# Top-32 attention and an ELU feed-forward block: the distance from threshold to largest score is formed on GpSimd in steps 0 to 7 as well

## The chip, the cores and the metric

The kernel runs on one core of a Trainium2 chip. The core's engines run beside each other and wait for one another by semaphores: PE (TensorE, matrix products and transposes; PEld is its weight load), DVE (VectorE), ACT (ScalarE), POOL (GpSimd) and SP (SyncE, which here only starts DMA transfers). Each engine works off its own instructions strictly in the order in which they stand in its queue. The metric is the device time of one execution in microseconds.

## The reference

Eight batches of eight heads, 576 positions, head dimension 64, float32. In every row of scores only the 32 largest take part in the softmax. The heads are then laid side by side as a (4608, 512) matrix, which goes through a feed-forward block of width 2048 with an ELU between its two products.

```python
scores = scale * np.matmul(q, k.transpose(0, 1, 3, 2))
kth = np.partition(scores, -top_k, axis=-1)[..., -top_k:-top_k + 1]
scores = np.where(scores >= kth, scores, -1000000000.0)
scores = scores - np.max(scores, axis=-1, keepdims=True)
attn = np.exp(scores)
attn = attn / (np.sum(attn, axis=-1, keepdims=True) + 1e-09)
attn_out = np.matmul(attn, v)
x = attn_out.transpose(0, 2, 1, 3).reshape(B * S, H * D)
h = x @ w_in
g = np.where(h > 0.0, h, np.exp(np.minimum(h, 0.0)) - 1.0)
out = g @ w_out
```

The weights arrive as float64 and are turned into float32 on the chip.

## The kernel before

**Steps.** The attention is cut into 144 steps. A step takes up to 128 query rows of two heads (the last 64 rows of a batch are paired over four heads), so that it has two rows of work, i = 0 and 1, each a tile of 128 x 576 scores. A step goes through these stations:

- `scores` (L302, L310): PE forms the scores in PSUM, ACT copies them scaled to `sc`. This runs two steps ahead.
- `select_row` (steps 0 to 7: L321, L325, L331) or `select` (later: L344, L349, L356): DVE finds the 32 largest of each row with four `max` instructions of eight values each, and three `match_replace` between them that blot out what was found. The first `max` leaves the largest score in `u.first`, the last one the threshold, the 32nd largest, in `u.last`.
- `mask` (L374 to L376): the gap, threshold minus largest score, one number per partition, is formed in a 128x1 tile. Then ACT applies a Prelu with the threshold as bias (L375) and an exponential with the gap as bias (L376). The two together give exp(score - largest) above the threshold and 0 below it; the exponential also sums the row into `den`.
- `normalise` (L386 to L393): POOL forms the reciprocal of the sum with five small instructions and scales both rows.
- `turn` (L412, L413): PE transposes the weights, ACT copies them to `et`. `attend` and `finish` (L438, L465): PE multiplies with v, and ACT copies the result to `xT`.

When all heads of a block of tokens are there, its feed-forward work is cut into pieces: `hidden` (L510 on PE, L520, L523 and L525 on ACT, the -1 of the ELU in L482 on DVE) and `project` (L535 on PE). `feed` hands them out four times a step by a running account of cost and due time.

**Weights.** `decode_piece` turns the 32 pieces of the weights into float32. A piece passes four stages in successive calls: ACT (L173, L174), then a clamp on POOL (L179) and the sign on ACT (L182), then a shift on DVE (L188), then an add on POOL (L192). SP loads the raw piece three calls ahead (L153) into one of seven buffers, so that each load waits for an add that frees its buffer. `hook` runs one call; `select_row` calls it twice per row, that is four times a step, so that decoding lies almost wholly in steps 0 to 7, with the rest in step 8.

**Order.** In steps 0 to 7 (`n < tight`, with tight = 8) a step's two rows come one after the other. For each the program issues: the first two `max`, for row 1 the normalisation and the transposes of the step before, a share of feed-forward pieces, the rest of the selection with its two decode calls, and then `mask` for that same row. These instructions are not bound to that order: the Tile framework's planner arranges the instructions of each engine by program order and by when their inputs are ready. From step 8 on (`manual_schedule` at L688) the order written in the program is kept on PE, ACT, DVE and POOL; there `mask` belongs to the step before, and its two rows are called at L697 and L705.

`mask` takes the engine that forms the gap as an argument, with GpSimd as default. The call in steps 0 to 7 (L684) passes VectorE; the two later calls pass nothing. Gap tiles have four buffers, so a gap can be written once the exponential four gaps before has read its own.

Of the kernel before, what the change touches and what calls it, by code (L numbers as in the profile page):

```python
# [9 lines left out]
ALU = mybir.AluOpType  # L10
# [71 lines left out]
def kernel(  # L82
# [9 lines left out]
    nc = tc.nc  # L92
# [191 lines left out]
    def turn_qk(whole=False):  # L284
        while turning:
            if next(turning[0], turning) is turning:
                turning.pop(0)
            elif not whole:
                return
# [3 lines left out]
    def scores(u):  # L293

        u.sc = scpool.tile([P, 2, S], FP32, tag="sc", name="sc")
        q0 = QUERIES + u.t.qt * P
        for half in range(2):
            for h, i, rows in u.heads:
                kq = kqT[u.t.b, h // 2]
                part = slice(i * D, (i + 1) * D)  # L300
                k0 = (KEYS if i == 0 else 0) + half * HS
                nc.tensor.matmul(  # L302
                    wide[i][rows, half, 0:HS],
                    kq[part, q0 : q0 + u.t.ql],
                    kq[part, k0 : k0 + HS],
                    start=True,
                    stop=True,
                )
        for i in range(2):
            nc.scalar.activation(  # L310
                u.sc[:, i, :].rearrange("p (a s) -> p a s", a=2),
                wide[i][:, :, 0:HS], AF.Copy, scale=scale,
            )

    def select_row(u, i):
        if i == 0:
            u.first = small.tile([P, 2, 8], FP32, tag="m1", name="m1")
            u.last = small.tile([P, 2, 8], FP32, tag="m4", name="m4")
        sc = u.sc[:, i, :]
        m = u.first[:, i, :]  # L320
        nc.vector.max(m, sc)  # L321
        wk = wkpool.tile([P, S], FP32, tag=f"wk{i}", name="wk")
        cur = sc
        for r in range(TOP_K // 8 - 1):
            nc.vector.match_replace(wk[:], m, cur, TAKEN)  # L325
            cur = wk[:]
            if r < TOP_K // 8 - 2:
                m = small.tile([P, 8], FP32, tag=f"m{i}", name="m")[:]
            else:
                m = u.last[:, i, :]  # L330
            nc.vector.max(m, cur)  # L331
            if r > 0:
                hook()
            if r != 1:
                yield
# [21 lines left out]
            hook()  # L357
            yield

    def mask(u, i, engine=nc.gpsimd):  # L360

        if u.masked:
            return
        if i == 0:
            u.den = small.tile([P, 2], FP32, tag="den", name="den")  # L370
        u.masked = i == 1
        sc, low, top = u.sc[:, i, :], u.last[:, i, 7:8], u.first[:, i, 0:1]
        gap = small.tile([P, 1], FP32, tag="gap", name="gap")
        engine.tensor_tensor(gap[:], low, top, ALU.subtract)  # L374
        nc.scalar.activation(sc, sc, AF.Prelu, scale=-1.0, bias=low, alpha=1.0 / STEEP)  # L375
        nc.scalar.activation(  # L376
            sc, sc, AF.Exp, scale=-STEEP, bias=gap[:], accum_out=u.den[:, i : i + 1]
        )

    def normalise(u):  # L380

        if u.normal:
            return
        u.normal = True
        den = small.tile([P, 2], FP32, tag="dene", name="dene")
        nc.gpsimd.tensor_scalar_add(den[:], u.den[:], EPS)  # L386
        rec = small.tile([P, 2], FP32, tag="rec", name="rec")
        nc.gpsimd.tensor_tensor(rec[:], den[:], power[:], ALU.pow)
        nc.gpsimd.tensor_tensor(den[:], den[:], rec[:], ALU.mult)
        nc.gpsimd.tensor_scalar(den[:], den[:], -1.0, 2.0, ALU.mult, ALU.add)  # L390
        nc.gpsimd.tensor_tensor(rec[:], rec[:], den[:], ALU.mult)
        for i in range(2):
            nc.gpsimd.tensor_scalar(  # L393
                u.sc[:, i, :], u.sc[:, i, :], rec[:, i : i + 1], 1.0, ALU.mult, ALU.mult
            )
# [26 lines left out]
    def attend(g):  # L422
        t = g.tiles[0]
        ps = ps_t.tile([P, JP], FP32, tag="t", name="avps")
        n = P if t.rem else sum(x.ql for x in g.tiles)
        for k in range(2 if t.rem else 1):
            hp = 2 * g.hp + k if t.rem else g.hp
            vt = vT[t.b, hp]
            for c in range(J + 1):
                for i in range(2):  # L430
                    chunk = J if c == J else i * (J + 1) + c
                    w = g.et[:, chunk, :, :].rearrange("p a q -> p (a q)")
                    cols = slice(0, n)
                    if t.rem:
                        c0 = R * (k if i == 0 else 1 - k)
                        w = w[:, c0 : c0 + R]
                        cols = slice(k * R, (k + 1) * R)
                    nc.tensor.matmul(  # L438
                        ps[i * D : (i + 1) * D, cols],
                        vt[:, 2 * J + i if c == J else i * J + c, :],  # L440
                        w,
                        start=(c == 0),
                        stop=(c == J),
                    )
        if t.rem:
            finish(t.block, 2, slice(2 * g.hp, 2 * g.hp + 2), t.cols,
                   ps[:, 0:n].rearrange("p (a q) -> p a q", a=2))
            return
        c0 = 0
        tiles = list(g.tiles)  # L450
        while tiles:
            blk, lo, parts = tiles[0].block, tiles[0].cols.start, 0
            while tiles and tiles[0].block is blk:
                parts += 1
                hi = tiles.pop(0).cols.stop
            finish(blk, parts, g.hp, slice(lo, hi), ps[:, c0 : c0 + hi - lo])
            c0 += hi - lo
# [165 lines left out]
    def feed(n, share):  # L623

        place[0] += 1
        close_gates(2)
        fed["at"] = max(fed["at"], n)
        ahead = [(w - fed["sum"]) / (x - fed["at"]) for x, w in due if x > fed["at"]]
        if ahead:
            fed["over"] += max(0.0, share * min(ahead))  # L630
        fed["at"] += share
        while ffn and decoded[0] >= ffn[0][1] and 0.5 * ffn[0][0] <= fed["over"]:
            cost, _, piece = ffn.pop(0)
            fed["over"] -= cost
            fed["sum"] += cost
            piece()
# [22 lines left out]
    def step(n):  # L659
        return steps[n] if 0 <= n < NS else None  # L660
# [3 lines left out]
    for n in range(NS + 3):  # L664
        for fn, args in todo.pop(n, []):
            fn(*args)
        ahead, cur, prev, done = step(n + 2), step(n), step(n - 1), step(n - 2)
        if n < tight:
            turn_qk(True)
            scores(ahead)  # L670
            for i in range(2):
                passes = select_row(cur, i)
                next(passes)
                if i == 0:
                    while closing:
                        attend(closing.pop(0))
                elif prev:
                    normalise(prev)
                    turn(prev, main)
                    turn(prev, rest)  # L680
                    turn(prev, other)
                feed(n, 0.25)
                next(passes)
                mask(cur, i, nc.vector)  # L684
                feed(n, 0.25)
            continue
        if n == tight:
            ctx.enter_context(tc.manual_schedule(engines=engines))  # L688
        passes = select(cur) if cur else iter(range(4))
        if ahead:  # L690
            scores(ahead)
        while closing:
            attend(closing.pop(0))
        next(passes)
        feed(n, 0.25)
        if prev:
            mask(prev, 0)  # L697
        turn_qk()
        next(passes)
        feed(n, 0.25)  # L700
        if done:
            turn(done, main)
            turn(done, rest)
        if prev:
            mask(prev, 1)  # L705
        next(passes)
        feed(n, 0.25)
        if done:
            turn(done, other)
        next(passes)  # L710
        if prev:
            normalise(prev)
        feed(n, 0.25)
        turn_qk(True)
# [36 lines left out]
```

## Time and profile before

| | us |
|---|---|
| median of four runs | 1664.47 (1663.52 to 1665.56) |
| the profiled execution | 1665.56 |
| its span, first to last instruction | 1663.8 |
| busy: PE, DVE, ACT, POOL | 1594.7, 1504.3, 1163.5, 579.2 |
| gaps (L374) on DVE: 16, from 25.9 to 127.4 | 8.33 busy |
| gaps (L374) on POOL: 272, from 149.9 to 1570.9 | median 0.191 each |

In the lines that follow, times are microseconds from the start of the span unless marked ns. A line of the stage table gives the stretch, its length, the busy time and the number of instructions of PE, PEld, DVE, ACT and POOL, then the granted TensorE clock as a share of full speed, the mean busy share of the DMA engines, and GB/s. A line of waits reads: engine and line that waited, whom for, total us, times, longest. A line of the chain has start, length and what ran; a line of the timeline has start, length, engine, line, operation, output and input, and in brackets the idle time before it with what ended it. A group of instructions of a line gives the durations in ns as min/median/max.

### The profile page before, as it was taken

How to read it: one execution, taken by the hardware profiler on the slowest of the kernel's cores; microseconds unless marked ns; L12 is line 12 of the kernel's file. 1: busy time of each engine (PE TensorE's matmuls, PEld its weight loads, DVE VectorE, ACT ScalarE, POOL GpSimd, SP SyncE). 2: the span in 40 equal slices, each digit the busy share in tenths (PEclk: the TensorE clock that was granted, in tenths of full speed). 3: DMA queues.
4: the chain of work that ended last, by engine and by line, in shares of the span. 5: the costliest groups of instructions: out<-in, count | busy, mean ns of one | idle time of the engine just before them, and what ended most of it. 6: DMA issues, size and time to landing. Idle time of an engine off the chain costs nothing.

```text
span 1663.8 us, 25650 instructions
## 1 busy us (share of the span) xinstructions
PE 1594.7 (96%) x8528; PEld 1031.1 (62%) x8528; DVE 1504.3 (90%) x3060; ACT 1163.5 (70%) x2377; POOL 579.2 (35%) x1415
## 2 busy tenths in 40 slices
PE   5579999999999999999999999999999999999999
PEld 3366777667574767656566676755557575755564
DVE  5898999999999999999999999999999999998500
ACT  5998777668685867678667676768758585857521
POOL 2775333333333333333333233333333333332200
PEclk9678999999999999999999999999999999999999
DMA  7540110001100210011100111001200101000000
GB/s 212 177 138 7 29 48 25 7 15 44 48 1 7 50 37 22 1 28 37 42 14 1 50 32 32 1 15 42 50 13 1 29 14 29 7 7 7 7 13 13
DMA packets 101124, 56.19 MB, mean 34 GB/s; under 512 B 84096, under 2 KB 92288, under 8 KB 100992
## 3 DMA queue, kind: packets, MB, share of 16 engines
q1 hardware_dynamic: 99792, 54.26, 11.7%
q8 instruction: 68, 1.11, 0.3%
q14 instruction: 64, 0.52, 0.1%
q10 hardware_dynamic: 1200, 0.30, 0.1%
HBM read 45.09 MB, written 9.44 MB: 33 GB/s over the span
## 4 chain that ended last, share of the span: by engine, by line
PE 62%; DVE 27%; ACT 5%; issue 1%; POOL 0%; DVEq 0%; ACTq 0%
PE ops L535 22%; PE hps L510 21%; DVE wk L349 12%; DVE m L356 10%; PE avps L438 7%; PE scps L302 6%; PE eps L412 5%; DVE m L344 3%; DVE gT L482 1%; PE qkps L272 1%; ACT sc L376 1%; PE scps L412 1%; ACT sc L375 1%; ACT et L413 1%; ACT raw L182 0%
## 5 line engine op out<-in xcount | busy, mean ns | idle before, releaser
L356 DVE MAX8 m<-wk 128x8 f32<-128x576 f32 x816 | 575.0, 746 | 0.0
L510 PE MATMUL hps<-xT,w_in 128*128 128x256 f32 (+2 forms) x2432 | 547.6, 374 | 12.8 <-ACT xT L465 10.7
L535 PE MATMUL ops<-w_out,gT 128*128 128x512 f32 x1152 | 523.0, 598 | 0.0
L510 PEld LDWEIGHTS hps<-xT,w_in 128*128 128x128 f32 x2432 | 405.9, 193 | 109.5 <-issue 24.2
L349 DVE MATCH_REPLACE8 wk<-m,wk 128x576 f32<-128x576 f32 x544 | 399.5, 741 | 0.0
L535 PEld LDWEIGHTS ops<-w_out,gT 128*128 128x128 f32 x1152 | 208.6, 190 | 233.1 <-issue 220.9
L386 POOL TENSOR_SCALAR dene<-den 128x2 f32<-128x2 f32 x144 | 35.4, 246 | 807.8 <-ACT sc L376 807.5
L375 ACT ACTIVATE sc<-sc,m 128x576 f32<-128x576 f32 x288 | 226.8, 788 | 39.6 <-DVE m L356 39.4
L376 ACT ACTIVATE sc<-sc,gap 128x576 f32<-128x576 f32 x288 | 224.0, 778 | 37.0 <-POOL gap L374 13.6
L310 ACT ACTIVATE sc<-scps 128x576 f32<-128x576 f32 x288 | 174.0, 659 | 77.2 <-PE scps L302 77.1
L393 POOL TENSOR_SCALAR sc<-sc,rec 128x576 f32<-128x576 f32 x288 | 220.7, 777 | 14.9
L302 PE MATMUL scps<-kqT 64*128 64x288 f32 (+1 forms) x1280 | 203.1, 441 | 19.3 <-ACT et L413 9.0
L413 ACT COPY et<-eps 128x512 f32<-128x512 f32 x288 | 166.8, 580 | 70.5 <-PE eps L412 70.2
L438 PE MATMUL avps<-et,vT 128*64 128x256 f32 (+2 forms) x2080 | 195.8, 330 | 4.7 <-ACT et L413 4.4
L349 DVE MATCH_REPLACE8 wk<-m,sc 128x576 f32<-128x576 f32 x272 | 199.8, 742 | 0.0
L412 PEld LDWEIGHTS eps<-ident,sc 128*128 128x128 f32 x1152 | 143.2, 143 | 81.6 <-issue 49.3
L344 DVE MAX8 m<-sc 128x8 f32<-128x576 f32 x272 | 191.1, 743 | 0.0
L482 DVE SCALAR_TENSOR_TENSOR gT<-n,gT 128x512 f32<-128x512 f32 (+1 forms) x132 | 99.8, 756 | 100.6 <-ACT n L525 100.6
L412 PE MATMUL eps<-ident,sc 128*128 128x128 f32 x1152 | 175.2, 277 | 13.6 <-POOL sc L393 11.8
L438 PEld LDWEIGHTS avps<-et,vT 128*64 128x64 f32 x2080 | 123.6, 142 | 80.7 <-issue 27.0
L302 PEld LDWEIGHTS scps<-kqT 64*128 64x128 f32 (+1 forms) x1280 | 108.2, 182 | 90.8 <-issue 44.7
L520 ACT ACTIVATE n<-hps 128x512 f32<-128x512 f32 (+1 forms) x156 | 88.1, 565 | 80.1 <-PE hps L510 76.6
(50 smaller groups left out, 1117.9 us busy)
## 6 DMA issues: line engine op xcount, KB each, us to landing
kin<-in_k_dram SPq DMA_DIRECT2D x64, 128.0 KB, 2.9
raw<-in_moe_w_in_dram SPq DMA_DIRECT2D x16, 512.0 KB, 5.1
vT<-in_v_dram SPq DMA_DIRECT2D x64, 128.0 KB, 2.3
raw<-in_moe_w_out_dram SPq DMA_DIRECT2D x16, 512.0 KB, 3.5
out_dram<-osb SPq DMA_DIRECT2D x32, 256.0 KB, 2.3
qin<-in_q_dram SPq DMA_DIRECT2D x62, 128.0 KB, 2.9
kin<-in_k_dram SPq DMA_DIRECT2D x32, 32.0 KB, 2.6
vT<-in_v_dram SPq DMA_DIRECT2D x64, 16.0 KB, 2.2
```

The source lines that it names most:

```text
L302: nc.tensor.matmul(wide[i][rows, half, 0:HS], kq[part, q0 : q0 + u.t.ql], kq[part, k0 : k0 + HS], start=True, stop=True,)
L344: nc.vector.max(found[i], cur[i])
L349: nc.vector.match_replace(wk[i], found[i], cur[i], TAKEN)
L356: nc.vector.max(found[i], cur[i])
L375: nc.scalar.activation(sc, sc, AF.Prelu, scale=-1.0, bias=low, alpha=1.0 / STEEP)
L376: nc.scalar.activation(sc, sc, AF.Exp, scale=-STEEP, bias=gap[:], accum_out=u.den[:, i : i + 1])
L393: nc.gpsimd.tensor_scalar(u.sc[:, i, :], u.sc[:, i, :], rec[:, i : i + 1], 1.0, ALU.mult, ALU.mult)
L412: nc.tensor.transpose(ps[:, c * P : (c + 1) * P], sc[:, c0 : c0 + P], ident[:])
L413: nc.scalar.copy(g.et[:, chunks, u.at, :], ps[:, 0 : n * P].rearrange("p (c q) -> p c q", c=n),)
L438: nc.tensor.matmul(ps[i * D : (i + 1) * D, cols], vt[:, 2 * J + i if c == J else i * J + c, :], w, start=(c == 0), stop=(c == J),)
L510: nc.tensor.matmul(blk.h[:, f % bank, :], w_in[:, i, f * P : (f + 1) * P], blk.xT[:, i, 0:n_tok], start=(i == 0), stop=(i == NC - 1),)
L535: nc.tensor.matmul(blk.o[:], blk.gT[f // NG][:, f % NG, s * P : (s + 1) * P], w_out[:, f, :], start=(f == 0), stop=(f == NF - 1),)
```

## The change

The call in steps 0 to 7 no longer names an engine, and the argument is gone: all 288 gaps are formed on GpSimd. Sixteen 128x1 subtractions (two rows in each of eight steps) go from DVE's queue to POOL's. Nothing is computed differently.

```diff
-    def mask(u, i, engine=nc.gpsimd):
+    def mask(u, i):
...
         gap = small.tile([P, 1], FP32, tag="gap", name="gap")
-        engine.tensor_tensor(gap[:], low, top, ALU.subtract)
+        nc.gpsimd.tensor_tensor(gap[:], low, top, ALU.subtract)
         nc.scalar.activation(sc, sc, AF.Prelu, scale=-1.0, bias=low, alpha=1.0 / STEEP)
         nc.scalar.activation(
             sc, sc, AF.Exp, scale=-STEEP, bias=gap[:], accum_out=u.den[:, i : i + 1]
         )
...
                 feed(n, 0.25)
                 next(passes)
-                mask(cur, i, nc.vector)
+                mask(cur, i)
                 feed(n, 0.25)
```

## The prediction

> **What bounds the kernel now.** I read the page's busy times first, then busy time by stage, then the waits of the stage in which the edited instructions run, then the chain of work that ended last.
>
> ```profile
> PE 1594.7 (96%) x8528; PEld 1031.1 (62%) x8528; DVE 1504.3 (90%) x3060; ACT 1163.5 (70%) x2377; POOL 579.2 (35%) x1415
> ```
>
> Averages put PE first, but the edit touches only steps 0 to 7, and the instructions of its line tell where these lie:
>
> ```profile
> L374 POOL TENSOR_TENSOR gap<-m,m x272: 182/191/887, 149.9 to 1570.9; 128x1 f32<-128x1 f32 x136
> L374 DVE TENSOR_TENSOR gap<-m,m x16: 143/152/1266, 25.9 to 127.4; 128x1 f32<-128x1 f32 x16
> ```
>
> 272 of the 288 gaps are on POOL already; the 16 that move run from 25.9 to 127.4 us. The table of stages (busy us of PE, PEld, DVE, ACT, POOL in each) shows who is full there:
>
> ```profile
> 20.00:40.00 20.00, 13.95 (x56) 8.61 (x55) 16.16 (x37) 12.13 (x26) 5.20 (x13) 0.83 0.75 241
> 40.00:60.00 20.00, 7.64 (x41) 5.02 (x40) 14.84 (x31) 20.00 (x35) 14.15 (x19) 0.70 0.36 114
> 60.00:80.00 20.00, 15.55 (x64) 10.46 (x63) 19.36 (x40) 20.00 (x34) 16.12 (x20) 0.53 0.74 214
> 80.00:100.00 20.00, 14.97 (x69) 11.41 (x70) 19.96 (x41) 20.00 (x36) 16.04 (x25) 0.66 0.55 177
> 100.00:120.00 20.00, 15.56 (x116) 12.81 (x113) 20.00 (x37) 20.00 (x38) 13.75 (x18) 0.91 0.40 133
> 120.00:140.00 20.00, 16.08 (x88) 12.12 (x89) 12.29 (x26) 20.00 (x36) 12.97 (x17) 0.67 0.08 27
> 140.00:160.00 20.00, 20.00 (x91) 10.59 (x90) 20.00 (x43) 13.69 (x26) 10.79 (x22) 1.00 0.04 14
> ```
>
> ACT is at 20.00 of 20 from 40 to 140 us; DVE looks as full from 60 to 120, but part of that is time in which it is held (below), and it has idle time on both sides. The waits between 39.5 and 140 us settle it. ACT has one:
>
> ```profile
> ACT sc L310 <- PE scps L302: 0.4, 1, 0.4
> ```
>
> DVE waits for POOL and ACT (answer for 20 to 140 us), which trail ACT:
>
> ```profile
> DVE w_in L188 <- POOL w_in L179: 9.5, 6, 5.3
> DVE w_out L188 <- POOL w_out L179: 4.8, 2, 2.9
> DVE gT L482 <- ACT n L525: 2.9, 2, 2.1
> ```
>
> The chain shows how this stage hands over to the next: ACT in it, and from 136.77 DVE, let go by ACT's exponential (L525).
>
> ```profile
> 135.23 0.50 ACT n L520
> 135.73 0.49 ACT gT L523
> 136.22 0.53 ACT n L525
> 136.74 0.02 issue
> 136.77 0.69 DVE gT L482
> 137.46 1.46 DVE wk L349 x3
> ```
>
> From there DVE and PE have almost no idle time, first DVE and then PE carrying the chain to the end. So what the change is worth is how far it moves the instant 136.77.
>
> **Removed from DVE.** 16 instructions, 8.33 us busy by the stage table for their line. The timeline shows ten of about 0.15 us and six that were held: 1.25, 1.26, 1.25, 1.27, 1.26 and 0.56 us, 6.85 in all. Beside the third, on POOL and then DVE:
>
> ```profile
> 73.88 1.53 POOL L192 TENSOR_TENSOR w_in<-w_in,raw 128x512 int32<-128x512 int32 x1
> ```
> ```profile
> 74.17 1.25 DVE L374 TENSOR_TENSOR gap<-m,m 128x1 f32<-128x1 f32 x1
> ```
>
> POOL's add ends at 75.41, the gap at 75.42: a 128x1 operation stands still until POOL is done. An ordinary one delays the next DVE instruction by 0.07 us (67.70 to 67.78 on the timeline), a held one by its length less 0.08. So DVE gets 10 x 0.07 + 6.85 - 6 x 0.08 = 7.1 us back. On the path to 136.77 this is worth nothing: after its last selection work DVE already sits idle for 2.93, 1.88 and 2.08 us (before its instructions at 131.95, 134.26 and 136.77), 6.9 us, because POOL's clamp (L179) and ACT's L525 are not there yet. Those waits become about 14 us. The cover is ACT, whose order of instructions ahead of L525 contains no DVE result that is late: the exponential that reads the gap (L376) starts 2.9 us after the gap's end for the first two gaps, and 4.4 us or more for all later ones (61.63 against 66.06 is the closest). If ACT were not full, up to 7.1 us would come through.
>
> **Added to POOL.** 16 x 0.19 = 3.1 us, about 4.5 with some 0.09 between instructions as the timeline has it. POOL is busy for 72.05 of the 97 us from 39.5 to 136.5, so the work fits; in that stretch POOL is let go again and again by ACT (L173, L182, L376), so a lag does not add up from step to step. The Trainium skill, GPSIMD Engine Reference, Engine selection, puts elementwise two-input work on VectorE because GpSimd is about 2x slower. The rows here say 191 against 152 ns, 1.26x, for this tiny shape; by the rule the moved work would be 16 x 0.30 = 4.9 us, which fits the same idle time, so the forecast would not change.
>
> **The wait it adds.** A gap on POOL waits for the last DVE max (L331) of its row, and POOL runs in order: behind it are the normalisation of the step before (L386 to L393), the clamp L179 and the add L192. Who waits for these: PE's transposes and then ACT's copy L413; DVE's shift L188; SP's weight loads (L153), with the key, query and value loads behind them on SP.
> - In program order the gap of a step's first row stands just ahead of L386, after two adds L192. Max ready (end of its row on DVE's timeline) against POOL free (end of the second add), steps 2 to 7: 51.36 and 53.15; 67.45 and 66.82; 80.60 and 80.69; 93.96 and 94.71; 106.58 and 111.36; 121.48 and 127.16. Only one is late, by 0.6 us, and with the gap itself L386 moves from 67.00 to about 67.8, inside the margin of 1.3 below. The others add 0 to 0.28.
> - The gap of the second row stands behind that row's two adds; the max is ready 2.1 us (73.27 and 75.41) to 9.4 us (126.40 and 135.84) before POOL is free. It costs 0.28 us ahead of an L179 that mostly waits for ACT anyway. So placed, every gap still ends 4.2 us or more ahead of its exponential (61.9 against 66.06).
> - Margin of ACT's L413 over the end of the transposes, step by step: 0.5 to 1.2 us (about 58.6), 1.3 to 1.6 (72.6), 1.7 to 2.0 (86.6), 2.8 (118.4) and 1.8 to 2.7 (133.1); at 100.6 PE was itself late with L510, and POOL had 1.0 to 1.7 in hand. In the step with 0.5, L386 at 53.55 was waiting for ACT's L376, and the gap fits ahead of it (53.2 to 53.4). So 0.
> - Weight loads: the add that frees a buffer ends about 15 us before ACT reads the load put there (59.29 against 74.44; 73.09 against 88.44), and landing takes 3.5 to 5.1 us. So 0.
> - At 25.9 us, before ACT is full, POOL is idle until its add at 27.34, and the exponentials start at 28.99 and 29.75. Even behind that add (28.63) the two gaps end by 29.2. So 0, at most 0.1.
>
> Bounds for the added wait as a whole: the steady stage shows POOL waiting for DVE's max before a gap 84 times, 79.4 us together, 0.95 on average, 3.3 at most. At 0.95 + 0.19 twice a step, 2.3 us, less a margin of 1.4, over six steps, is 5.3 us; with the smallest margin of 0.5, 10.7. The low end is 0. I take 0, since the maxima read off this very stage are nearer than those of a stage where POOL has little else to do.
>
> **Order.** Steps 0 to 7 are put in order by the planner, not by hand: on DVE a max of step 8 (L344, 124.66) already stands before step 7's last max (125.65). Taking an instruction from DVE and putting it on POOL may shuffle the neighbours. What matters is whether a decode group of ACT (L173, L174, L182; 128.00 to 130.21, 2.2 us) changes sides with L525: 2.2 us for one group, 4.4 for a pair, of either sign. ACT has a backlog and works it off in program order, so I take 0.
>
> **Sum.** Saved on the path 0, added 0. The profiled execution took 1665.56 us, span 1663.8 and 1.76 around it; it is the slowest of the four shown, 1.09 over the median. Zero added to the median gives 1664.5.
>
> **Rivals.**
> - *POOL's queue becomes the wait* (slower). Place: the gap ahead of L386. Price 5.3 us by the mean wait: 1669.8; 10.7 by the smallest margin: 1675.2. It decides once L386 comes over 1.4 us late in most steps, or 0.5 in the tightest. For: POOL is 80% busy from 60 to 100 and would wait for a DVE that is nearly full; against: the ready times above, and DVE gets earlier.
> - *The planner's order shifts.* A pair of decode groups before or behind L525: 1668.9 or 1660.1; one group, 1666.7 or 1662.3, is inside what counts as the same.
> - *The DVE time comes through* (faster). For: the chain runs over DVE from 73.83 to 90.66, with gaps of 1.25, 0.07 and 1.27 on it, 2.6 us; all relief is 7.1. That gives 1661.9 down to 1657.4. Against: at 90.66 it steps to ACT, which had no idle time there, so the release was a tie.
>
> **Chances.** No change 0.58 (single groups included). POOL's queue 0.13. Order to the slow side 0.14, to the fast side 0.08. DVE time 0.07. What a measurement of this kernel can tell from no change is about 0.2%, 3.3 us. Slower by more: 0.13 + 0.14 = 0.27. Faster: 0.15. For the range I leave out the 10.7 and 7.1 ends: from 1660.0 (a pair of groups gained) to 1671.0 (the queue by its mean wait, with 1.2 over it). The likeliest case alone spans 1662.3 to 1666.7.
>
> **What the new profile would show.** All 288 gaps on POOL; DVE waits before its instructions near 132 to 137 us of about 14 us instead of 6.9; ACT without idle time from 39.5 to 137; the hand-over to DVE within 2 us of 136.77; POOL waits for L331 only around one or two gaps. ACT idle before L413 or L376, or long POOL waits for L331, would mean the queue rival; another sequence of ACT's instructions between 120 and 140 the order rival; a hand-over 2.6 us or more earlier with the same sequence the DVE rival. Wrong would be, above all, the assumption that the planner leaves ACT's sequence alone.

## The result, and the profile after

The changed kernel takes 1666.44 us (median of 33 runs, 1665.33 to 1668.65), the kernel before 1664.41 us beside it (53 runs, 1662.6 to 1667.28). The ratio is 1.0010, with a 95% interval of 1.0006 to 1.0015: a loss of about 2.0 us by the medians, 1.0 to 2.5 by the interval. That is inside the 3.3 us that the prediction called no change, and inside its range; but the interval leaves out one, so there is a loss to explain, and the predicted mechanism contained none. The profiled execution took 1667.09 us, its span 1665.3.

The same views as before, now of the changed kernel. The page's busy times:

```profile
PE 1594.6 (96%) x8528; PEld 1032.2 (62%) x8528; DVE 1499.7 (90%) x3044; ACT 1163.6 (70%) x2377; POOL 581.5 (35%) x1431
```

DVE has 16 instructions and 4.6 us less, POOL 16 instructions and 2.3 us more. The instructions of the edited line, and the part of that answer that tells what POOL waited for before them:

```profile
L374 POOL TENSOR_TENSOR gap<-m,m x288: 181/191/888, 25.4 to 1572.4; 128x1 f32<-128x1 f32 x144
...
  DVE m L331: 16.9, 10
```

All 288 gaps are on POOL. The moved ones made it stand still for 16.9 us, ten times, until DVE's last maximum of the row was there. The table of stages (columns as in the table of before):

```profile
40.00:60.00 20.00, 7.68 (x41) 5.11 (x41) 12.91 (x28) 20.00 (x34) 14.70 (x21) 0.62 0.35 116
60.00:80.00 20.00, 15.62 (x64) 10.47 (x63) 18.35 (x39) 20.00 (x34) 16.46 (x25) 0.53 0.72 206
80.00:100.00 20.00, 14.52 (x63) 10.78 (x63) 19.37 (x37) 20.00 (x36) 14.27 (x25) 0.66 0.60 183
100.00:120.00 20.00, 15.30 (x113) 13.28 (x114) 15.96 (x32) 19.34 (x37) 14.85 (x21) 0.91 0.33 107
120.00:140.00 20.00, 16.37 (x88) 12.41 (x89) 12.24 (x21) 19.37 (x35) 15.79 (x21) 0.67 0.17 53
```

ACT, full to the last hundredth before, now has two holes, 0.66 us after 100 and 0.63 us after 120. The waits of ACT between 39.5 and 140 us name them:

```profile
ACT et L413 <- PE eps L412: 1.3, 2, 0.7
ACT sc L310 <- PE scps L302: 0.4, 1, 0.4
```

The second line was there before; the first is new. The waits of DVE from 20 to 145 us show where its relief went:

```profile
DVE w_in L188 <- POOL w_in L179: 12.1, 7, 5.0
DVE w_out L188 <- POOL w_out L179: 11.9, 8, 4.0
DVE gT L482 <- ACT n L525: 0.5, 1, 0.5
```

DVE is busy 76.68 us from 39.5 to 136.5 instead of 83.22, and it waits for POOL's clamp for 24.0 us instead of 14.3. What it was spared it spent waiting for POOL. The chain of work that ended last, in the stretch before the hand-over (start, length, what ran):

```profile
128.88 1.54 POOL w_out L192
130.41 0.08 issue
130.50 0.56 POOL dene L386
...
132.78 0.77 POOL sc L393
133.55 0.04 issue
133.59 1.13 PE eps L412 x4
134.72 0.02 issue
134.75 0.02 ACT et L413
...
136.74 0.50 ACT n L520
137.24 0.49 ACT gT L523
137.73 0.53 ACT n L525
138.25 0.02 issue
138.28 1.15 DVE gT L482
```

Before, this stretch was ACT throughout. Now the chain comes from POOL: its add, the normalisation, PE's transposes, and only then ACT. The hand-over is at 138.28 instead of 136.77, and the first DVE instruction behind it takes 1.15 us instead of 0.69.

**The stall itself.** POOL's timeline (start, length, engine, line, operation, output and input, idle time before it and what ended it) at both places where ACT was starved a few microseconds later:

```profile
94.01 1.28 POOL L192 TENSOR_TENSOR w_out<-w_out,raw 128x512 int32<-128x512 int32 x1
97.71 0.19 POOL L374 TENSOR_TENSOR gap<-m,m 128x1 f32<-128x1 f32 x1 [2.42 <-DVE m L331]
97.98 0.23 POOL L386 TENSOR_SCALAR dene<-den 128x2 f32<-128x2 f32 x1
...
127.80 0.29 POOL L374 TENSOR_TENSOR gap<-m,m 128x1 f32<-128x1 f32 x1 [2.68 <-DVE m L331]
128.18 0.61 POOL L179 TENSOR_SCALAR w_out<-w_out 128x512 f32<-128x512 f32 x1
128.88 1.54 POOL L192 TENSOR_TENSOR w_out<-w_out,raw 128x512 int32<-128x512 int32 x1
130.50 0.55 POOL L386 TENSOR_SCALAR dene<-den 128x2 f32<-128x2 f32 x1
```

These are the gaps of the *second* rows of steps 5 and 7. In the program each stands behind the normalisation of the step before (L386 to L393); the planner has put it ahead of it, in step 5 directly, in step 7 with a clamp and an add between. The first row's gap of step 5 stands at 91.74, before the add at 94.01. At 95.3 POOL could have begun to normalise. Instead it waits 2.42 us for a maximum that only the gap needs. PE and ACT follow (the timelines of PE and of ACT, cut to the waiting instructions):

```profile
100.76 0.66 PE L412 MATMUL eps<-ident,sc 128*128 128x128 f32 x4 [1.08 <-POOL sc L393]
```

```profile
101.45 0.59 ACT L413 COPY et<-eps 128x512 f32<-128x512 f32 x1 [0.66 <-PE eps L412]
...
134.75 0.59 ACT L413 COPY et<-eps 128x512 f32<-128x512 f32 x1 [0.63 <-PE eps L412]
```

**From 1.4 us to 2.0 us.** DVE's timeline from the hand-over on:

```profile
138.28 1.15 DVE L482 SCALAR_TENSOR_TENSOR gT<-n,gT 128x512 f32<-128x512 f32 x1 [0.55 <-ACT n L525]
...
142.14 1.28 DVE L188 TENSOR_SCALAR w_out<-w_out 128x512 uint32<-128x512 uint32 x1
```

Before they took 0.69 and 0.41. POOL now runs late enough for its decode adds to fall on them: an add (L192) of 1.53 us starts at 137.35. So DVE begins the selection of step 9 not 1.4 but 2.8 us later (counted as in the table below). From there DVE works without a break, and the delay shows once more near 190 us, where ACT waits for a maximum of DVE and PE for ACT. The lines are the waits of ACT from 180 to 195 us and of PE from 140 to 260 us, of the changed kernel and then of the kernel before:

```profile
ACT sc L375 <- DVE m L356: 3.0, 1, 3.0
```

```profile
PE eps L412 <- ACT kqT L278: 2.5, 1, 2.5
```

```profile
ACT sc L375 <- DVE m L356: 1.0, 1, 1.0
```

```profile
PE eps L412 <- ACT kqT L278: 0.5, 1, 0.5
```

PE loses 2.0 us there: it is idle for 9.47 us between 140 and 400 instead of 6.97. That the delay lasts to the end is seen from the ends of the traces, compared in the section on the prediction.

**How the profiled executions are compared.** Single profiled spans cannot be compared as they are, for two reasons. The loading of the first inputs takes different times, so that ACT's full stretch begins anywhere from 38.1 to 41.3 us (the two profiled spans of the changed kernel, 1665.3 and 1664.2, differ mostly by that). And in all but two of the executions the granted clock drops to about 0.83 or below in some 10 us slice after 300 us. So all positions below are counted from the start of ACT's first L173 after 36 us, and total times are medians. A ratio is against executions of the kernel before made beside that kernel (medians 1664.16 to 1664.41). *Stretch* is from there to ACT's fourth L525, which releases the hand-over; *step 9* is the start of DVE's first maximum (L344) of that step; *PE* is the wait of L412 shown above; the last column is the start of the normalisation (L386) issued in steps 5, 6 and 7.

| kernel | median us | ratio, 95% interval | stretch | step 9 | PE | L386 in steps 5, 6, 7 |
|---|---|---|---|---|---|---|
| before | 1664.41 | | 95.87 | 106.33 | 0.5 | 54.96, 71.39, 87.20 |
| changed | 1666.44 | 1.0010, 1.0006 to 1.0015 | 97.45 | 109.10 | 2.5 | 57.84, 74.67, 90.36 |
| e5_after_again | 1665.94 | 1.0013, 1.0004 to 1.0022 | 97.45 | 109.09 | 2.5 | 57.83, 74.67, 90.35 |
| e1_no_gap | 1664.71 | 1.0004, 0.9995 to 1.0013 | 95.92 | 106.30 | 0.2 | 54.97, 71.12, 86.09 |
| e2_first_rows_pool | 1664.30 | 1.0001, 0.9992 to 1.0010 | 96.31 | 107.96 | 1.8 | 56.32, 72.91, 89.13 |
| e3_second_rows_pool | 1664.30 | 1.0000, 0.9992 to 1.0009 | 95.97 | 106.35 | 0.5 | 55.06, 71.95, 88.09 |
| e4_gap_behind_normalise | 1664.73 | 1.0002, 0.9993 to 1.0011 | 95.77 | 106.24 | 0.2 | 55.20, 71.94, 86.50 |
| e6_extra_pool_gap | 1664.28 | 1.0001, 0.9992 to 1.0010 | 95.74 | 106.40 | 0.5 | 55.52, 72.58, 88.45 |
| e9_behind_in_step_5 | 1664.19 | 1.0001, 0.9992 to 1.0010 | 96.08 | 107.70 | 1.8 | 55.21, 73.28, 88.99 |
| e10_behind_in_step_7 | 1665.21 | 1.0006, 0.9997 to 1.0015 | 96.60 | 108.32 | 1.6 | 57.85, 74.68, 89.50 |
| e7_eight_decodes_on_dve | 1660.19 | 0.9979, 0.9970 to 0.9988 | 93.47 | 103.89 | 0.3 | 54.52, 69.67, 84.80 |
| e12_eight_decodes_again | 1660.41 | 0.9978, 0.9968 to 0.9987 | 93.45 | 103.86 | 0.4 | 54.47, 69.60, 84.72 |
| e8_sixteen_decodes_on_dve | 1663.23 | 0.9994, 0.9985 to 1.0002 | 94.44 | 106.18 | 2.2 | 53.81, 69.40, 85.83 |
| e11_decode_on_dve_gap_behind | 1662.06 | 0.9988, 0.9979 to 0.9997 | 92.90 | 103.29 | 0.2 | 53.34, 68.61, 84.62 |

The changed kernel, profiled twice, has the same positions to 0.01 us; e7 and e12, one kernel too, agree to 0.08. So a few tenths of a microsecond in these columns mean something, while a time with an interval of plus or minus 1.5 us can hardly tell 0 from 2. The verdicts below rest on the positions first.

### The profile page after: what moved, and what is told of

Its sections match the earlier page's. It is cut to its first block, busy times and chain, and to the rows that moved or that the text cites. A ratio compares the mean times of both kernels' runs of the same rounds, so it can differ in the third digit from the quotient of the medians.

```text
span 1665.3 us, 25645 instructions
## 1 busy us (share of the span) xinstructions
PE 1594.6 (96%) x8528; PEld 1032.2 (62%) x8528; DVE 1499.7 (90%) x3044; ACT 1163.6 (70%) x2377; POOL 581.5 (35%) x1431
## 4 chain that ended last, share of the span: by engine, by line
PE 67%; DVE 19%; ACT 5%; issue 1%; POOL 1%; ACTq 0%; DVEq 0%; POOLq 0%
PE ops L535 25%; PE hps L510 21%; DVE wk L349 8%; PE avps L438 8%; DVE m L356 7%; PE scps L302 6%; PE eps L412 5%; DVE m L344 2%; DVE gT L482 1%; ACT sc L376 1%; PE qkps L272 1%; ACT sc L375 1%; ACT et L413 1%; PE scps L412 1%; ACT n L520 0%
## 5 line engine op out<-in xcount | busy, mean ns | idle before, releaser
L386 POOL TENSOR_SCALAR dene<-den 128x2 f32<-128x2 f32 x144 | 35.7, 248 | 808.3 <-ACT sc L376 807.9
L375 ACT ACTIVATE sc<-sc,m 128x576 f32<-128x576 f32 x288 | 226.9, 788 | 43.1 <-DVE m L356 42.8
L393 POOL TENSOR_SCALAR sc<-sc,rec 128x576 f32<-128x576 f32 x288 | 220.1, 775 | 15.0 <-POOL rec L391 0.2
L413 ACT COPY et<-eps 128x512 f32<-128x512 f32 x288 | 166.6, 579 | 71.4 <-PE eps L412 71.3
L412 PEld LDWEIGHTS eps<-ident,sc 128*128 128x128 f32 x1152 | 144.5, 145 | 89.1 <-issue 49.0
L412 PE MATMUL eps<-ident,sc 128*128 128x128 f32 x1152 | 177.2, 280 | 20.9 <-POOL sc L393 17.1
L344 DVE MAX8 m<-sc 128x8 f32<-128x576 f32 x272 | 191.3, 744 | 0.0
L482 DVE SCALAR_TENSOR_TENSOR gT<-n,gT 128x512 f32<-128x512 f32 (+1 forms) x132 | 101.7, 771 | 97.1 <-ACT n L525 97.1
```

The source lines that it names most:

```text
L344: nc.vector.max(found[i], cur[i])
L393: nc.gpsimd.tensor_scalar(u.sc[:, i, :], u.sc[:, i, :], rec[:, i : i + 1], 1.0, ALU.mult, ALU.mult)
L412: nc.tensor.transpose(ps[:, c * P : (c + 1) * P], sc[:, c0 : c0 + P], ident[:])
L413: nc.scalar.copy(g.et[:, chunks, u.at, :], ps[:, 0 : n * P].rearrange("p (c q) -> p c q", c=n),)
```

## The experiments

Theories: (1) POOL's queue: the second rows' gaps stop POOL ahead of the normalisation. (2) DVE's order: the planner also rearranged DVE once the 16 instructions were gone, and that is what is late. (3) The relief of DVE is worth something, and hides part of the loss.

**e1_no_gap**: the changed kernel without the gap in steps 0 to 7. The exponential there takes the threshold as bias, so the largest score is not subtracted in those steps. Neither engine has the 16 instructions.

```diff
-    def mask(u, i):
+    def mask(u, i, early=False):
...
-        gap = small.tile([P, 1], FP32, tag="gap", name="gap")
-        nc.gpsimd.tensor_tensor(gap[:], low, top, ALU.subtract)
+        gap = low if early else small.tile([P, 1], FP32, tag="gap", name="gap")[:]
+        early or nc.gpsimd.tensor_tensor(gap, low, top, ALU.subtract)
...
-            sc, sc, AF.Exp, scale=-STEEP, bias=gap[:], accum_out=u.den[:, i : i + 1]
+            sc, sc, AF.Exp, scale=-STEEP, bias=gap, accum_out=u.den[:, i : i + 1]
...
-                mask(cur, i)
+                mask(cur, i, True)
```

> Steps 0 to 7 leave out the gap: the exponential takes the threshold itself as bias, so the largest score is not subtracted in those steps (the softmax ratios are the same). Neither DVE nor POOL forms a gap there. The orders of PE and SP are those of the kernel before. Theory 1 (POOL's gaps wait for DVE's max, the normalisation behind them comes late, and ACT stands still at L413): no ACT idle time before L413 from 39.5 to 137 us, hand-over (DVE's L482 ahead of its first L349) back at 136.8 +- 0.3, time 1664.4 +- 0.8. Theory 2 (DVE's new sequence, without the gaps, is what is slower): ACT idle 1 us or more, hand-over 138 or later, about 1666.4. Theory 3 (DVE's 7.1 us come through once POOL is not burdened): hand-over 134 or earlier, 1662 or less.

The stretch is 95.92 against 95.87 before, DVE's step 9 at 106.30 against 106.33, and ACT has no wait for PE's transposes. DVE without the 16 gaps gains nothing, so theory 3 falls. Removing them from POOL removes the whole loss.

**e2_first_rows_pool** and **e3_second_rows_pool**: only the first, or only the second, rows' gaps move to POOL; the others stay on DVE.

```diff
-                mask(cur, i)
+                mask(cur, i, nc.gpsimd if i == 0 else nc.vector)
```
```diff
-                mask(cur, i)
+                mask(cur, i, nc.vector if i == 0 else nc.gpsimd)
```

> In steps 0 to 7 the gap of the first row is formed on POOL and that of the second row on DVE. ACT, PE and SP keep their order; on POOL each such gap stands two adds ahead of the normalisation. Theory 1: the first row's max is early enough, so L386 moves by 0.3 us or so, no ACT idle time before L413, hand-over 136.8 to 137.1, time 1664.4 +- 0.8. Theory 2 (another sequence on DVE is slower): hand-over 138 or later, about 1666.

> The reverse: first rows on DVE, second rows on POOL. On POOL the second row's gap stands directly ahead of the normalisation in steps 6 and 7 only (in the changed kernel in 5, 6 and 7). Theory 1: POOL waits 1 to 3 us for the max there, L386 comes 2 to 3 us late; step 6 has the margin (2.8 us), step 7 loses about 0.8: hand-over 137.3 to 138.0, time 1665 to 1666. Theory 2: hand-over as in the first-rows variant.

Both missed: the loss does not belong to one half. First rows alone make POOL wait 15.4 us in seven stops, make L386 about 1.4 to 1.9 us late, and cost 0.44 us of stretch and 1.6 us at step 9. Second rows alone make it 0.1, 0.6 and 0.9 us late and cost 0.10 us of stretch and nothing at step 9: with the first rows' gaps on DVE, the planner put the second row's gap ahead of the normalisation only in steps 6 and 7. The times tell neither from zero. Halves of a moved queue are not halves of the change, because with each edit the planner chooses new places for the gaps on POOL, and a new order on DVE.

**e4_gap_behind_normalise**, which decides between theories 1 and 2: the changed kernel, with the second row's gap bound behind the last instruction of the normalisation.

```diff
-    def mask(u, i):
+    def mask(u, i, behind=None):
...
-        nc.gpsimd.tensor_tensor(gap[:], low, top, ALU.subtract)
+        with tc.issue_after(behind.scaled.ins) if behind else ExitStack():
+            nc.gpsimd.tensor_tensor(gap[:], low, top, ALU.subtract)
...
-            nc.gpsimd.tensor_scalar(
+            u.scaled = nc.gpsimd.tensor_scalar(
...
-                mask(cur, i)
+                mask(cur, i, prev if i == 1 else None)
```

> The changed kernel, all gaps on POOL, but the planner is made to issue the second row's gap behind the normalisation of the step before. Instructions, engines and DVE's work are those of the changed kernel; only POOL's order differs. Theory 1: L386 back to within 0.5 us of its times before (95.0, 111.4, 127.3), no ACT idle time before L413, hand-over 136.8 to 137.1, time 1664.4 +- 0.8. If the order on POOL does not matter: hand-over 138.3 and 1666.4 as in the changed kernel.

The sequences of ACT, PE, SP and DVE are the same as in the changed kernel; only POOL's differs. POOL's timeline at the place shown above:

```profile
92.72 1.29 POOL L192 TENSOR_TENSOR w_out<-w_out,raw 128x512 int32<-128x512 int32 x1
94.10 0.28 POOL L386 TENSOR_SCALAR dene<-den 128x2 f32<-128x2 f32 x1
...
97.67 0.61 POOL L179 TENSOR_SCALAR w_out<-w_out 128x512 f32<-128x512 f32 x1
98.36 0.19 POOL L374 TENSOR_TENSOR gap<-m,m 128x1 f32<-128x1 f32 x1
```

The normalisation starts as soon as the add is out of the way, and the gap, 4.3 us later, finds its maximum ready. The stretch is 95.77, step 9 is at 106.24, and PE's wait is 0.2: all of the loss is gone with DVE's order unchanged, so theory 2 falls. The times say the same: eight of the eleven executions are faster than the fastest of the changed kernel's 33 (1665.33 us). Of POOL's waits from 20 to 140 us this much is left:

```profile
POOL gap L374 <- DVE m L331: 13.2, 7, 4.7
```

So POOL still waits for 13.2 us, and these waits cost nothing. DVE's timeline at the hand-over is back too:

```profile
135.53 0.69 DVE L482 SCALAR_TENSOR_TENSOR gT<-n,gT 128x512 f32<-128x512 f32 x1 [2.77 <-ACT n L525]
...
138.92 0.41 DVE L188 TENSOR_SCALAR w_out<-w_out 128x512 uint32<-128x512 uint32 x1
```

**e5_after_again**: the changed kernel once more, without an edit.

> The changed kernel once more, beside the others of this call on the same chip. Theory 1 (POOL's gaps in front of the normalisation): ACT idle before L413 about 1.3 us in all, ACT's stretch from its first L173 after 36 us to its fourth L525 longer by about 1.5 us than before (97.45 against 95.87), time 1 to 2.5 us over the kernel before.

1665.94 us, ratio 1.0013 with an interval that leaves out one: the loss repeats.

**e6_extra_pool_gap**: the kernel before, with a second gap on POOL beside the one on DVE. Nothing reads it.

```diff
         engine.tensor_tensor(gap[:], low, top, ALU.subtract)
+        if engine is nc.vector:
+            spare = small.tile([P, 1], FP32, tag="spare", name="spare")
+            nc.gpsimd.tensor_tensor(spare[:], low, top, ALU.subtract)
```

> The kernel before with one more instruction per row in steps 0 to 7: POOL forms the gap too, into a tile that nobody reads; the exponential still reads DVE's gap. DVE, ACT, PE and SP have the kernel before's instructions in its order; on POOL the extra ones stand ahead of the normalisation about as in the changed kernel (second rows: one add ahead of it in step 5 and in step 7, directly ahead in step 6). So the wait on POOL is added alone, with DVE's work and order untouched. Theory 1: ACT idle before L413 0.5 to 2 us, ACT's stretch 96.5 to 98, time 1 to 3 us over the kernel before. Theory 2 (DVE's new sequence costs it, not POOL's wait): ACT's stretch 95.9, time as before.

A miss: it was meant to show the stall by itself, and there was none. POOL waits almost as much as in the changed kernel:

```profile
POOL spare L374 <- DVE m L331: 14.7, 9, 4.7
```

but its timeline shows another order in step 5 (the first three lines), and the second rows' stops in steps 6 and 7 (the last two):

```profile
92.11 0.19 POOL L374 TENSOR_TENSOR spare<-m,m 128x1 f32<-128x1 f32 x1 [1.03 <-DVE m L331]
...
93.62 0.28 POOL L386 TENSOR_SCALAR dene<-den 128x2 f32<-128x2 f32 x1
...
97.90 0.49 POOL L374 TENSOR_TENSOR spare<-m,m 128x1 f32<-128x1 f32 x1
...
110.41 0.19 POOL L374 TENSOR_TENSOR spare<-m,m 128x1 f32<-128x1 f32 x1 [1.04 <-DVE m L331]
...
125.03 0.19 POOL L374 TENSOR_TENSOR spare<-m,m 128x1 f32<-128x1 f32 x1 [2.00 <-DVE m L331]
```

In step 5 the wait is ahead of the first row's gap; the second row's, at 97.90, stands behind the normalisation. In steps 6 and 7 the second row's gap does stand ahead of the normalisation, but after its stops L386 is only 1.2 us late in each, which the prediction's margins there (2.8, and 1.8 to 2.7) cover; in step 5 it is 0.6 us late. ACT has no wait for PE, and the stretch is 95.74. Waits of 14.7 us are free here, and the mean wait is no price at all: what counts is in front of which instruction a wait falls, and whether that instruction comes later than its margin allows.

**e9_behind_in_step_5** and **e10_behind_in_step_7**: as e4, but the gap is bound in one step only.

```diff
-                mask(cur, i, prev if i == 1 else None)
+                mask(cur, i, prev if i == 1 and n == 5 else None)
```
```diff
-                mask(cur, i, prev if i == 1 else None)
+                mask(cur, i, prev if i == 1 and n == 7 else None)
```

> The changed kernel, with the second row's gap made to follow the normalisation in step 5 alone; the other engines keep the changed kernel's order, POOL keeps it in the other steps. Two delays in series (theory 1: one stop of ACT before L413 near 100 us, a second near 134): the first goes, the second stays, ACT's stretch half way, 96.5 to 96.9 (95.8 with all behind, 97.45 with none). If the stop in step 7 alone decides, because what is lost in step 5 is waited for there anyway: 97.3 to 97.5.

> The same for step 7 alone. Delays in series: the stop near 100 us stays, the one near 134 goes, ACT's stretch 96.5 to 96.9. If step 7 alone decides: 95.8 to 96.0. If step 5 alone decides: 97.3 to 97.5. DVE's start of step 9 comes later than with all behind by this and by what POOL's adds hold it at the hand-over (1.4 us in the changed kernel, where POOL lags, 0 where it does not); PE's wait for ACT's L278 near 190 us grows by DVE's delay less 0.3 to 0.5 us, and the time with it: 1664.5 to 1665.5.

Step 5 alone cured takes 1.37 us off the stretch (97.45 to 96.08), more than expected: ACT's stall of step 7 goes too, because that step's normalisation now comes 1.4 us earlier (88.99 against 90.36) and stays inside its margin. Step 7 alone cured takes off 0.85, as expected. Together the two would be 2.2, against 1.68 for e4, so the two stops are not independent: without the first, ACT does not stop at the second either. In both variants DVE's L482 and L188 at the hand-over still take about 1.2 us each, and step 9 stays 1.4 and 2.0 us late. The held instructions go with POOL's lag, not with ACT's stall.

**e7_eight_decodes_on_dve**, repeated as **e12_eight_decodes_again**: the kernel before, with every fourth conversion L174 taken from ACT, the full engine, to DVE, which waits.

```diff
-        nc.scalar.activation(lo.bitcast(FP32), lo, AF.Copy, scale=2.0**-35, bias=2.0**17)
+        if i % 4 == 3:
+            nc.vector.tensor_scalar(
+                lo.bitcast(FP32), lo, 2.0**-35, 2.0**17, ALU.mult, ALU.add
+            )
+        else:
+            nc.scalar.activation(
+                lo.bitcast(FP32), lo, AF.Copy, scale=2.0**-35, bias=2.0**17
+            )
```

> The kernel before, with the second conversion (L174) of every fourth weight piece on DVE instead of ACT: eight instructions of 0.57 us less on ACT, eight more on DVE. It tests whether ACT alone sets the hand-over. If ACT does and DVE has the idle time (15 us before): ACT's stretch to its fourth L525 shorter by 4 to 4.6 us, hand-over by as much earlier, time 3 to 4.6 us below the kernel before. If DVE or POOL bound it just as well: within 1 us of before.

> The variant with eight conversions on DVE and the early gaps on DVE, once more: if it beats both kernels for good, 1659.5 to 1661 again, 3 to 5 us under the kernel before of this call.

1660.19 and 1660.41 us, ratios of 0.9979 (0.9970 to 0.9988) and 0.9978 (0.9968 to 0.9987): 3.8 to 4.0 us faster than the kernel before, and better than both kernels of this case. This says what the stage is limited by: DVE's time is worth nothing, ACT's is worth something. The busy times from 39.5 to 136.5 us:

```profile
39.50:136.50 97.00, 70.72 (x373) 53.17 (x374) 90.04 (x178) 96.09 (x164) 73.11 (x96) 0.65 0.43 138
```

The stretch is 2.4 us shorter where about 4 were expected. Seven of the eight conversions lie in it; at some 0.57 us of ACT's queue each that is 4.0, and ACT now has 0.8 us of waits that it did not have (0.5 for DVE's last maximum before L375, 0.3 for PE before L413). The remaining 0.8 is not accounted for. Nor is it settled why the time fell by more than the stretch. Counted as in the table, the last instruction ends at 1619.3 in e7 and e12 and at 1622.3 to 1622.6 in e1, e3 and e4, so the traces show 3.0 to 3.3 of the 3.8 to 4.0 us. These two are also the only profiled executions without a drop of the granted clock, but that is not the reason: the drop that e1, e3 and e4 have, at 330 to 340 us, costs about a tenth of a microsecond (last section).

**e8_sixteen_decodes_on_dve** and **e11_decode_on_dve_gap_behind**: e4 with every second conversion on DVE (`i % 2 == 1`), and with every fourth (`i % 4 == 3`).

> All gaps on POOL with the second row's behind the normalisation (as in the variant of the first call), and the second conversion (L174) of every second weight piece on DVE: ACT has 16 x 0.57 = 9.1 us less to do, DVE 16 more of about 0.5 to 1.3 us and no gaps. If ACT alone set the hand-over, 9 us earlier and 1655 to 1657; DVE has 15 us idle time and 7 back from the gaps, so about 10 of extra work should fit, but with DVE near full I expect half to be lost: 1658 to 1661.

> All gaps on POOL, the second row's behind the normalisation, and the second conversion (L174) of every fourth weight piece on DVE. The variant with eight conversions on DVE and the gaps on DVE too had DVE 90 of 97 us busy, and took 1660.2. Without the gaps DVE has about 7 us less. If DVE's load limits what ACT's relief is worth: 1657 to 1659.5. If PE and ACT set it alone: 1660 +- 0.8.

Both missed. Sixteen give 1663.23 us (0.9985 to 1.0002): ACT waits for DVE's maxima (1.8 us), for the gaps on POOL (1.8) and for PE (1.2), so the relieved engine waits for the loaded one. e11 gives 1662.06 (0.9979 to 0.9997), slower than e7, although its stretch (92.90) and step 9 (103.29) are the earliest of all. Its profiled execution shows the clock at 0.82 from 320 to 330, 0.84 from 330 to 340 and 0.83 from 690 to 700 us. It falls behind e7 only around the last of these: two of ACT's copies (L465) are 42.17 us apart there (678.35 and 720.52) and 40.27 in e7 (680.56 and 720.83). That this drop is the cause was not tested, and since this execution (1660.94 us) is the fastest of the eleven, the median stays unexplained.

## Why the prediction was right in its time and wrong in a step

The time fell inside the range because the loss is smaller than the 3.3 us called no change, and not because the added wait was nothing. To that extent it was luck.

- **What bounds the stage** (ACT, and the worth of the change is the move of the hand-over): right. e1 shows that 7 us less on DVE are worth nothing, and e7 that ACT's time is worth something. What it missed is that the first instructions *behind* the hand-over count in the same way: they added 1.4 us of delay to 1.4.
- **Removed from DVE, worth nothing on the path**: right in the worth, wrong in the place. The waits did grow, from 14.3 to 24.0 us for POOL's clamp between 20 and 145 us, but ahead of many L188 rather than just before the hand-over. There the three waits that were 6.9 us came to 6.5 (4.04, 1.88 and 0.55), not 14. POOL's lag is not the reason: in e1, where POOL has no early gaps, they are 6.5 as well (1.34, 1.88 and 3.29). At most the growth of the clamp's waits from 20.3 us in e1 to 24.0 goes with the lag.
- **Added to POOL, fits in its idle time**: the busy time grew from 72.05 to 72.92 us in the stretch, and room was never the question.
- **The wait it adds, taken as 0**: this is the step that failed, at the sentence that "the gap of the second row stands behind that row's two adds". The ready times were read for positions that the planner did not choose. It put the second row's gap ahead of the normalisation in steps 5, 6 and 7, and in these steps the first row's gap ahead of that row's two adds instead of behind them. L386 came 2.9, 3.3 and 3.2 us late, where the prediction had allowed for at most 0.8. The margins explain what came of it. In step 5 the 1.0 to 1.7 us that POOL had in hand ahead of PE, and another 0.6 from the end of PE's transposes to ACT's copy (100.02 to 100.62 in the kernel before), left ACT idle for 0.66 us. In step 6 the margin of 2.8 us, with ACT itself late by then, absorbed the delay. In step 7 the margin of 1.8 to 2.7 did not, and ACT was idle for 0.63 us.
- **Order: ACT's sequence stays**: right. ACT, PE and SP run the same sequences as before. The planner did rearrange DVE, which did no harm (e4). On POOL everything but the gaps kept its order, and the place that the planner chose for the second rows' gaps is the loss.
- **The rivals.** POOL's queue is what happened, at 2.0 us instead of 5.3. The mean wait came out close (16.9 us over 16 gaps is 1.06, against 0.95), partly by luck, since POOL stopped for only ten of the sixteen, 1.69 us on average and 4.7 at most where the steady stage had shown 3.3; but a price of "mean wait less margin in every step" was the wrong form: e6 has nearly the same waits at no cost. A pair of decode groups changing sides with L525 did not occur. The DVE time did not come through.
- **The signs named**: POOL waits "around one or two gaps" were ten, and ACT idle before L413, named as the sign of the queue rival, was there. The hand-over did stay within 2 us of 136.77.

Shown are the place of the stop (e4, e9, e10 against the changed kernel), its removal with DVE's order kept, and that the relief is worth nothing (e1). The path from the hand-over to the end, over the held L482 and L188 and PE's wait near 190 us, is read from traces and was not varied by itself. It fits the changed kernel (+2.0 us at PE, +2.0 us in time), but e2 and e9 have 1.3 us of that wait and times that do not differ from before by more than their intervals of about plus or minus 1.5 us. So the exchange rate between step 9 and the end is not settled by the medians. The ends of the traces tell more. Seven profiled executions have the same single drop of the clock (0.83 from 330 to 340 us). Counted as in the table, their last instruction ends at 1622.3 (e3), 1622.6 (e1 and e4), 1623.4 (e2), 1623.6 (e9), 1624.2 (e10) and 1625.2 (e5, the changed kernel). So the 2.8 us by which step 9 is late in the changed kernel arrive at the end as 2.6 to 2.9, the 2.0 of e10 as 1.6 to 1.9, and the 1.4 and 1.6 of e9 and e2 as 0.8 to 1.3. These are single executions, one for each kernel.

## What to carry to other kernels

A tiny instruction that moves to another engine's queue costs what it stops there, not its duration: list what may stand behind it, ask of each whether it waits for the same late input, and do so for every place that a planner may choose, not only for the program's order. If the critical work behind it does not need that input, bind the small instruction behind it; here that took back all of the 1.6 us by which the stretch had grown, without moving anything else. And where one engine has no idle time, work taken from any other engine turns into waits; look at what the full engine could give away instead.

## What the runs showed of the hardware

- **Two-input work on DVE held by POOL.** Not only the 128x1 gaps: L482 took 1.15 us instead of 0.69, and L188 1.28 instead of 0.41, where one of POOL's adds (L192, 1.3 to 1.5 us) was under way when they came, as those that start at 137.35 and 141.85 in the changed kernel, and 0.69 and 0.41 where none was (e4, whose add starts at 139.08, after L188 at 138.92). For L188, which reads one input, the kernel before shows the same (1.49 us at 115.81, under an add from 115.72 to 117.02), but it is a coincidence in time that no run tested. For L482, which reads two inputs, this agrees with the Trainium skill, "SBUF — State Buffer", section "SBUF: two separate sides", by which the pair of ports that DVE and GpSimd share is held for a whole instruction by whichever of them started first. An engine that runs late can so lengthen work of another that does not wait for it.
- **Drops of the granted clock.** Profiled executions of nearly the same program show 10 us slices at 0.66 to 0.96, most often at 330 to 340 us, in some also near 510 to 530 or 700; e7 and e12 show none. What a slice costs depends on where it falls. Around 330 to 340 us, two of ACT's copies (L465) start 184.94 us apart in e7, without a drop (311.90 and 496.84), 185.02 in e4, at 0.83 (313.37 and 498.39), and 185.10 in the kernel before, at 0.66 (314.47 and 499.57): 0.1 to 0.2 us. Around 700 us, two later copies are 40.79 apart in e4, without a drop there (681.82 and 722.61), and 42.10 in the kernel before, at 0.83 (683.04 and 725.14): 1.3 us, more than half of the loss measured here. That is why single spans were not compared.
- **The loading phase** varied by 3.2 us between executions (38.1 to 41.3), and the positions behind it repeated to 0.01 us in the two executions of the changed kernel and to 0.08 us in e7 and e12.
